# Sampled and end key blocks in one score product, weight tiles moved ahead in the queue, and an order planned by forward and backward passes

## The chip, the cores and the metric

The kernel runs on one core of one Trainium2 chip. The metric is the device time of one execution in microseconds. Before the change the median of three runs is 842.47 us (842.19 to 844.38).

## The reference

Block-sparse attention feeds a two-layer expert with a piecewise activation. There are 4 batches, 8 heads, 768 positions and a head size of 64. Positions form 24 blocks of 32. A query of block i attends to blocks i-1, i and i+1, to blocks 0 and 23, and to three blocks drawn for i. Queries of blocks 0 and 23 attend to everything.

```
scores = where(mask, q @ k.T / 8, -1e9)
attn   = softmax(scores);  x = attn @ v            # 3072 tokens x 512
h      = x @ w_in                                  # 512 -> 2048
g      = where(h >= 1, h, where(h <= -1, 0, (h + 1)**2 / 4))
out    = g @ w_out                                 # 2048 -> 512
```

The weights arrive in float64 and q, k, v in float32.

## The kernel before

**Groups.** Each batch is cut into six groups of 128 query rows. Groups 0 to 4 of a batch hold four middle blocks each; the sixth, called mixed, holds blocks 21 and 22 and the two dense blocks 0 and 23. There are 24 groups, 4 of them mixed. Groups are gathered into nine chunks of (3, 2, 3, 3, 3, 3, 3, 2, 2) groups; the expert (the MoE steps) of a chunk runs over its rows while the attention of the next chunk is worked in between.

**Attention of a group.** A middle group has two score rounds, a mixed one has one. So there are 20 x 2 + 4 = 44 rounds, of which the first two chunks (five middle groups) hold 10 and the other chunks 34. `score_parts` issues a round: 16 products (4 query blocks, 2 head halves `e`, 2 head pairs), each product of 32 queries on a 64-row by 32-column part of TensorE, so that eight parts work side by side, into the two PSUM banks `sa` and `sb`. Each product is made three times over: with the three neighbour blocks out of `KN` (96 columns), with the three sampled blocks out of `KR` (96 columns), and with blocks 0 and 23 out of `KN` (64 columns). A float32 product is two instructions, so each of the three sections is 32 matmuls. A bf16 product with `mask` follows. All go through the helper `mm` (L193). Then VectorE takes minima (L378), ScalarE exponentials (L381), TensorE turns the probabilities (`turn`, L386), and `values` multiplies them with the value tiles `VA` and `VB`. The rows of the mixed group that attend to everything get `far_scores` over all 24 blocks and `far_values`.

**Sampled blocks.** GpSimd reads three block numbers per query block into registers and copies the blocks from `KN` to one of three buffers `KR` (six copies of 128 x 128 for two query blocks, L321). SyncE reads the same numbers and loads the value blocks into `VA` (six transfers, L328). `KN` holds all keys of one batch and has one buffer.

**Weights.** `convert` loads a tile of 128 x 512 float64 into one of four parts of `STG`, and makes of it two float32r tiles (high and low part): ScalarE (L249), four VectorE instructions (L250, L252, L254, L256), a ScalarE copy (L258), a GpSimd subtraction (L260). There are 16 tiles of `w_in`, which stay, and 16 of `w_out`, which also go out to DRAM and come back in every later chunk. All 32 conversions belong to the time up to the end of chunk 0's MoE steps. A MoE step is twelve matmuls into `h` (L591 to L593), the activation on ScalarE, GpSimd and VectorE (L596 to L604), and three matmuls per group into `oa` (L610 to L612).

**The order.** Nothing is issued as it is written down. `Plan.add` records each step with its engine, an estimated duration and a key (a due time made of hand-set constants such as `T0`, `P0`, `CONV0` and the `LEAD_` values). `Plan.order` plays the steps through once: whenever an engine is free it takes the ready step with the smallest key. The order in which steps were taken is the order in which instructions are issued, on each engine and on SyncE's one queue of transfers.

Of the kernel before, what the change touches and what calls it, by code (L numbers as in the profile page):

```python
# [9 lines left out]
F32 = mybir.dt.float32  # L10
# [10 lines left out]
NB, BLK, NR = 24, 32, 3  # L21
# [12 lines left out]
class Plan:  # L34
# [24 lines left out]

    def order(self):  # L60

        n = len(self.steps)
        left = [len(s[4]) for s in self.steps]
        users = [[] for _ in range(n)]
        for i, s in enumerate(self.steps):
            for d in s[4]:
                users[d].append(i)
# [7 lines left out]
        done, wire, out, begin, fin = [], 0.0, [], [0.0] * n, [0.0] * n  # L75
        busy = {e: 0.0 for e in free}
        while len(out) < n:
            best = None
            for e in free:
                t = free[e]  # L80
                if e == "SP" and len(done) >= LANES:
                    t = max(t, done[-LANES])
                while wait[e] and wait[e][0][0] <= t:
                    i = heapq.heappop(wait[e])[1]
                    heapq.heappush(avail[e], (self.steps[i][2], i))
                if not avail[e]:
                    if not wait[e]:
                        continue
                    t = wait[e][0][0]
                if best is None or t < best[0]:  # L90
                    best = (t, e)
            t, e = best
            while wait[e] and wait[e][0][0] <= t:
                i = heapq.heappop(wait[e])[1]
                heapq.heappush(avail[e], (self.steps[i][2], i))
            i = heapq.heappop(avail[e])[1]
            eng, dur, key, fn, deps, lat, size = self.steps[i]
            begin[i] = t
            free[e] = t + dur
            busy[e] += dur  # L100
            end = t + dur + lat
            if size:
                wire = max(wire, t + dur + 1.0) + size / 290e3
                end = wire + 0.8
                if e == "SP":
                    done.append(end)
            out.append(i)
            fin[i] = end
            for u in users[i]:
                left[u] -= 1  # L110
                ready[u] = max(ready[u], end)
                if not left[u]:
                    heapq.heappush(wait[self.steps[u][0]], (ready[u], u))
        self.begin, self.fin, self.busy, self.end = begin, fin, busy, max(free.values())
        return out


LANES = 8


@with_exitstack
def body(ctx, tc, q_t, k_t, v, samp, moe_w_in, moe_w_out, cst_in, out):
# [148 lines left out]
    def group(b, t, key, wide, lead):  # L271
# [20 lines left out]
        def at(x):  # L292
            return key + wide * x
# [9 lines left out]
        for hf in range(nh):  # L303
            n = half[0] % 3
            half[0] += 1
            slots.append(n)
            i0 = blocks[2 * hf]
            if fresh.get(n) != b:
                fresh[n] = b
                for name, tl, blk in (("va", VA[n], 0), ("vb", VB[n], NB - 1)):  # L310
                    src = v[b * S + blk * BLK:b * S + (blk + 1) * BLK].unsqueeze(1).to_broadcast([BLK, 2, DM])
                    load(at(0) - lead + 2.0 + hf, tl[96:128], src, (), [(name, n, "g")], size=131072)

# [4 lines left out]

            def keys(n=n, values_of=values_of):
                for m, val in enumerate(values_of(mybir.EngineType.Pool)):  # L320
                    POOL.tensor_copy(out=KR[n][:, m // NR, m % NR:m % NR + 1], in_=KN[:, bass.ds(val, 1)])  # L321

            pool(1.39 + 6 * 0.34, at(0) - 1.5 + hf, keys, ["sreg"] + [("kn", s) for s in range(6)], [("kr", n)])

# [4 lines left out]

            add("SP", 0.3 + 6 * 0.42, at(0) - lead + 3.5 + hf, gather, ["sreg"], [("va", n)], size=6 * 65536)  # L330
            src = bass.AP(v.tensor, (b * S + (i0 - 1) * BLK) * DM, [[DM, 96], [BLK * DM, 2], [1, DM]])
            load(at(0) - lead + 2.5 + hf, VB[n][0:96], src, (), [("vb", n)], size=393216)
        pool(0.75, at(0) - 0.5, lambda: POOL.tensor_scalar(out=q, in0=q, scalar1=-SCALE, scalar2=0.0, op0=ALU.mult, op1=ALU.add),
# [4 lines left out]

        kn_r = [("kn", s) for s in (range(6) if mixed else {0, 5, t, t + 1})]
        kr_r = [("kr", n) for n in slots]  # L340

        def score_parts(items):
# [11 lines left out]
            for e, p, col, quad, qs, i, c in items:  # L354
                go(e, quad, keys_at(col + 128, 3), q[64 * e:64 * e + 64, p, qs], KN[64 * e:64 * e + 64, i - 1:i + 2, p])
            for e, p, col, quad, qs, i, c in items:
                n, j = place(c)
                go(e, quad, keys_at(col, 3), q[64 * e:64 * e + 64, p, qs], KR[n][64 * e:64 * e + 64, j, :, p])
            for e, p, col, quad, qs, i, c in items:
                go(e, quad, lambda o: o[:, col:col + 256].rearrange("p (a s k) -> p a s k", a=2, k=BLK)[:, :, 3],  # L360
                   q[64 * e:64 * e + 64, p, qs], KN[64 * e:64 * e + 64, 0:NB:NB - 1, p])
            for e, quad, i in sorted({(x[0], x[3], x[5]) for x in items}, key=lambda x: (x[1], x[0])):
# [7 lines left out]
                if i in (1, NB - 2):  # L370
                    go(e, quad, both(4 if i == 1 else 6, 1), ones[es], never[es].unsqueeze(1).unsqueeze(2).to_broadcast([64, 2, 1, BLK]))

        score_reads = [qr, "mask", "ones"] + kn_r + kr_r
        va_r = [r for n in slots for r in (("va", n), ("va", n, "g"))]
        vb_r = [r for n in slots for r in (("vb", n), ("vb", n, "g"))]

# [20 lines left out]
        if not mixed:  # L397
            for rnd in range(2):
# [11 lines left out]
                for a in range(2):  # L410
                    p = 2 * rnd + a
                    bn, bk = ptbank()
                    pe(0.4, at(0.28 * rnd + 0.12 + 0.1 * a),
                       lambda a=a, bk=bk: turn(bk, [P[2 * a + e][:, h * 128:h * 128 + 128] for e in range(2) for h in range(2)]),
# [3 lines left out]
            def values():  # L418
                first = True
                for p in range(NP):  # L420
                    for e in range(2):
                        for hf in range(2):
                            for c in range(4):
                                n, j = place(c)
# [4 lines left out]
            pe(2.2, at(0.66), values, [("pt", p) for p in range(NP)] + va_r + vb_r, [on])  # L429

# [5 lines left out]
        else:  # L436
# [9 lines left out]
            for rho in range(2):  # L446
                pe(0.4, at(0.10 + 0.05 * rho),
                   lambda rho=rho: turn(ptb, [P[2 * rho + e][:, h * 128:h * 128 + 128] for e in range(2) for h in range(2)]),
# [3 lines left out]
            def near_values():  # L452
                first = True
                for rho in range(2):
                    for e in range(2):
                        for hf in range(2):
                            for u in range(2):
                                hd = 2 * (rho + 2 * u) + e
                                for c in range(2):
                                    n, j = place(c)  # L460
                                    quad = 2 * u + c
# [3 lines left out]

            pe(1.25, at(0.25), near_values, [("pt", 0), ("pt", 1)] + va_r + vb_r, [on])

# [81 lines left out]

        pe(0.4, k0 + 0.02 * wide, turn_back, ["xn", "cst"], [bn])  # L550
        pv = bk.rearrange("p (a c) -> p a c", a=NP)
# [12 lines left out]
    def moe(c, t0, p):  # L564
# [5 lines left out]
        for fi in range(NF):  # L570
# [23 lines left out]

            pe(0.7 * size[c], u, l1, x_r + [(("wi", fi // 4, k), w_) for k in range(4) for w_ in ("hi", "lo")], [hn])
            act(0.6, u, lambda r=r, h=h: ACT.activation(out=r, in_=h, func=AF.Relu, bias=half_c, scale=0.5),  # L596
# [16 lines left out]

            pe(0.7 * size[c], u + p * L2, l2, [("gh", n3), ("gl", ng)] + w_r, [("oa", t) for t in range(size[c])])
        for t in range(size[c]):
# [14 lines left out]

    fresh = {}
    constants()
# [9 lines left out]
    for c in range(NC):  # L642
# [93 lines left out]
```

## Time and profile before

| | |
|---|---|
| median of three runs | 842.47 us |
| the profiled execution's own time | 842.23 us |
| its span, first to last instruction | 840.4 us |
| TensorE matmul busy | 769.2 us, 92% |
| VectorE busy | 404.6 us, 48% |
| ScalarE busy | 387.5 us, 46% |
| GpSimd busy | 212.6 us, 25% |

The own time is 1.83 us above the span; the rest of the document counts in the span's microseconds from its start. Shares are means over stages with different limits, so the table says little on its own: the stages have to be read apart. PE stands for TensorE, DVE for VectorE, ACT for ScalarE, POOL for GpSimd, and SP (its queue: SPq) for SyncE.

### The profile page before, as it was taken

To read this page: it belongs to the slowest core of one execution; us is meant where nothing else is said; L and a number is where in the kernel's file an instruction comes from. 1 tells how busy PE (TensorE), PEld (TensorE's weight loads), DVE (VectorE), ACT (ScalarE), POOL (GpSimd) and SP (SyncE) were. 2 spreads that over 40 slices of the span, in tenths; PEclk is the share of its full clock that TensorE was granted. 3 is DMA by queue.
4 is the path that set the end of the run, shared out by engine and by line. 5 is a ranking of instruction groups with operands and counts; after the bars stand their busy time and mean duration, and the time that the engine had idled before them with its cause. 6 is when DMAs were issued, how large, how long until landed. Compare 5 with 4: busy or idle time off the path is not lost.

```text
span 840.4 us, 27419 instructions
## 1 busy us (share of the span) xinstructions
PE 769.2 (92%) x11376; PEld 665.4 (79%) x11376; DVE 404.6 (48%) x781; ACT 387.5 (46%) x959; POOL 212.6 (25%) x468
## 2 busy tenths in 40 slices
PE   4467669999989899999999999999999999999996
PEld 3356548788877788888888888888888798887995
DVE  2377989884454334434444344434433243444322
ACT  1365746555453334363435434364434343445542
POOL 2255464531422121014222111014223030110110
PEclk6598979999999999999999999999999999999999
DMA  6667779679656545666454745665454636353554
GB/s 189 214 179 224 236 221 330 232 250 298 218 182 168 176 143 170 194 217 195 122 161 150 223 137 165 200 216 195 134 175 159 187 111 195 125 166 121 160 196 151
DMA packets 63280, 157.24 MB, mean 187 GB/s; under 512 B 9652, under 2 KB 9908, under 8 KB 63156
## 3 DMA queue, kind: packets, MB, share of 16 engines
q1 hardware_dynamic: 63156, 155.49, 58.9%
q8 instruction: 89, 1.46, 0.7%
q14 instruction: 35, 0.29, 0.1%
HBM read 140.78 MB, written 14.68 MB: 185 GB/s over the span
## 4 chain that ended last, share of the span: by engine, by line
PE 78%; DVE 7%; DMA 4%; issue 4%; SPq 3%; ACT 2%; POOL 1%; ACTq 0%; POOLq 0%; DVEq 0%
PE h L591 10%; PE oa L610 10%; PE oa L611 10%; PE oa L612 9%; PE h L593 9%; PE h L592 9%; PE ob L193 6%; PE ptb L386 5%; PE sa L193 5%; PE sb L193 2%; SPq L328 2%; DVE stg L254 1%; DVE stg L256 1%; DMA va<-in_v_dram 1%; DMA stg<-in_moe_w_in_dram 1%
## 5 line engine op out<-in xcount | busy, mean ns | idle before, releaser
L598 POOL TENSOR_SCALAR gt<-r 128x384 f32<-128x384 f32 (+1 forms) x144 | 72.9, 506 | 480.6 <-ACT r L596 459.2
L591 PE MATMUL h<-x,wi 128*128 128x384 f32 (+1 forms) x536 | 182.3, 340 | 4.4 <-ACT r L596 2.9
L593 PE MATMUL h<-x,wi 128*128 128x384 f32 (+1 forms) x536 | 172.2, 321 | 0.0
L592 PE MATMUL h<-x,wi 128*128 128x384 f32 (+1 forms) x536 | 171.8, 321 | 0.0
L610 PE MATMUL oa<-w,gh 128*128 128x512 f32 x384 | 158.2, 412 | 10.0 <-ACT w L258 6.6
L611 PE MATMUL oa<-w,gh 128*128 128x512 f32 x384 | 153.6, 400 | 1.1 <-POOL w L260 1.1
L612 PE MATMUL oa<-w,gl 128*128 128x512 f32 x384 | 153.0, 399 | 0.0
L601 DVE SCALAR_TENSOR_TENSOR r<-r,gt 128x384 f32<-128x384 f32 (+1 forms) x144 | 77.3, 537 | 121.9 <-ACT r L600 121.4
L604 DVE TENSOR_TENSOR gl<-r,gh 128x384 fp32r<-128x384 f32 (+1 forms) x144 | 78.5, 545 | 119.2 <-PE oa L612 99.6
L603 ACT CAST gh<-r 128x384 fp32r<-128x384 f32 (+1 forms) x144 | 68.7, 477 | 118.1 <-DVE r L601 95.5
L591 PEld LDWEIGHTS h<-x,wi 128*128 128x128 f32 x536 | 101.0, 188 | 17.8 <-ACT r L596 5.9
L596 ACT ACTIVATE r<-h,half_c 128x384 f32<-128x384 f32 (+1 forms) x134 | 73.8, 551 | 88.9 <-PE h L593 84.1
L592 PEld LDWEIGHTS h<-x,wi 128*128 128x128 f32 x536 | 101.3, 189 | 2.0 <-issue 1.0
L593 PEld LDWEIGHTS h<-x,wi 128*128 128x128 f32 x536 | 101.0, 188 | 0.0
L600 ACT ACTIVATE r<-r 128x384 f32<-128x384 f32 (+1 forms) x144 | 70.4, 489 | 59.0 <-POOL gt L598 58.5
L610 PEld LDWEIGHTS oa<-w,gh 128*128 128x128 f32 x384 | 73.5, 191 | 25.1 <-ACT w L258 6.8
L321 POOL COPY kr<-kn 128x128 f32 x264 | 74.0, 329 | 60.7 <-PE sb L193 31.9
L612 PEld LDWEIGHTS oa<-w,gl 128*128 128x128 f32 x384 | 73.5, 191 | 16.5
L611 PEld LDWEIGHTS oa<-w,gh 128*128 128x128 f32 x384 | 73.7, 192 | 13.7 <-POOL w L260 2.0
L193 PE MATMUL sa<-kn,q 64*32 64x96 f32 (+2 forms) x1408 | 66.7, 259 | 5.9 <-issue 2.7
L381 ACT ACTIVATE p<-sa,nm 128x256 f32<-128x256 f32 x84 | 39.3, 471 | 68.6 <-DVE nm L378 66.0
L193 PE MATMUL sb<-kn,q 64*32 64x96 f32 (+2 forms) x1408 | 65.7, 259 | 0.0
(112 smaller groups left out, 1172.7 us busy)
## 6 DMA issues: line engine op xcount, KB each, us to landing
w<-wo_dram SPq DMA_DIRECT2D x128, 512.0 KB, 3.5
vb<-in_v_dram SPq DMA_DIRECT2D x44, 384.0 KB, 3.9
va<-in_v_dram SPq DMA_DIRECT2D x264, 64.0 KB, 2.8
stg<-in_moe_w_in_dram SPq DMA_DIRECT2D x16, 512.0 KB, 5.0
stg<-in_moe_w_out_dram SPq DMA_DIRECT2D x16, 512.0 KB, 4.2
wo_dram<-w SPq DMA_DIRECT2D x16, 512.0 KB, 4.6
q<-in_q_t_dram SPq DMA_DIRECT2D x24, 256.0 KB, 4.2
kn<-in_k_t_dram SPq DMA_DIRECT2D x24, 256.0 KB, 4.6
```

The costliest lines, as they stand in the source:

```text
L193: PE.matmul(out=o, lhsT=l, rhs=r, start=start, stop=True, skip_group_check=True)
L321: POOL.tensor_copy(out=KR[n][:, m // NR, m % NR:m % NR + 1], in_=KN[:, bass.ds(val, 1)])
L591: PE.matmul(out=h, lhsT=wi[:, j, 0, fs], rhs=x[:, j, 0, 0:nt], start=(j == 0), stop=False)
L592: PE.matmul(out=h, lhsT=wi[:, j, 0, fs], rhs=x[:, j, 1, 0:nt], start=False, stop=False)
L593: PE.matmul(out=h, lhsT=wi[:, j, 1, fs], rhs=x[:, j, 0, 0:nt], start=False, stop=(j == NP - 1))
L596: act(0.6, u, lambda r=r, h=h: ACT.activation(out=r, in_=h, func=AF.Relu, bias=half_c, scale=0.5), [hn, "half_c"], [("r", n2)])
L598: pool(0.55, u, lambda r=r, gt=gt: POOL.tensor_scalar(out=gt, in0=r, scalar1=2.0, scalar2=-1.0, op0=ALU.mult, op1=ALU.add), [("r", n2)], [ ...
L601: dve(0.56, u, lambda r=r, gt=gt: DVE.scalar_tensor_tensor(out=r, in0=r, scalar=1.0, in1=gt, op0=ALU.min, op1=ALU.max), [("gt", n2)], [("r ...
L604: dve(0.56, u, lambda r=r, gh=gh, gl=gl: DVE.tensor_tensor(out=gl, in0=r, in1=f(gh), op=ALU.subtract), [("r", n2), ("gh", n3)], [("gl", ng)])
L610: PE.matmul(out=oa[t], lhsT=gh[:, ts], rhs=w[:, 0], start=(fi == 0), stop=False)
L611: PE.matmul(out=oa[t], lhsT=gh[:, ts], rhs=w[:, 1], start=False, stop=False)
L612: PE.matmul(out=oa[t], lhsT=gl[:, ts], rhs=w[:, 0], start=False, stop=(fi == NF - 1))
```

## The change

It has three parts.

First, `KR` gets two more places: blocks 0 and 23 are copied beside the three sampled ones (`ends`, two copies of 128 x 256 whenever a buffer goes to another batch), and the sampled product and the product with blocks 0 and 23 become one of 160 columns. It is issued first, the neighbour product second. `KR` goes from three buffers to two. The value rows move to match: block 23 stands at the head of `VB` and the neighbours behind it. Numbers and sizes of transfers stay.

Second, the constants of the keys are set anew. `CONV0` goes from 7.6 to -20 and the lead of the first chunk's attention loads from 60 to 18.45, so that by the keys the first four `w_in` tiles come ahead of the first group's loads. Some estimated durations change too.

Third, `order` plays the steps through up to five times. After each forward pass a backward pass runs from the end to the start and gives every step a new key (how late it may begin); the forward pass with the earliest planned end is kept.

```diff
-    def order(self):
+    def run(self, key, deps, back):
...
+    def order(self):
+
+        deps = [s[4] for s in self.steps]
+        users = [set() for _ in deps]
+        for i, d in enumerate(deps):
+            for x in d:
+                users[x].add(i)
+        key, best = [s[2] for s in self.steps], None
+        for _ in range(PASSES):
+            got = self.run(key, deps, False)
+            if best is None or got[0] < best[0]:
+                best = got
+            ends = [-(got[2][i] + s[1]) for i, s in enumerate(self.steps)]
+            key = [-x for x in self.run(ends, users, True)[3]]
+        self.end, out, self.begin, self.fin = best
...
-    KR = ring(3, [128, 2, NR, NP, BLK], F32, "kr")
+    KR = ring(2, [128, 2, NR + 2, NP, BLK], F32, "kr")
...
-        add("SP", 0.35 * n, key, lambda: SP.dma_start(out=dst, in_=src), reads, writes, size=size)
+        add("SP", 0.47 * n, key, lambda: SP.dma_start(out=dst, in_=src), reads, writes, size=size)
...
+            if stale.get(kn) != b:
+                stale[kn] = b
+
+                def ends(kn=kn):
+                    for j in range(2):
+                        POOL.tensor_copy(out=KR[kn][:, j, NR:NR + 2], in_=KN[:, 0:NB:NB - 1])
+
+                pool(0.9, at(0) - 1.6 + hf, ends, [("kn", 0), ("kn", 5)], [("kr", kn, "g")])
...
             for e, p, col, quad, qs, i, c in items:
-                go(e, quad, keys_at(col + 128, 3), q[64 * e:64 * e + 64, p, qs], KN[64 * e:64 * e + 64, i - 1:i + 2, p])
+                (n, kn), j = place(c)
+                go(e, quad, keys_at(col, NR + 2), q[64 * e:64 * e + 64, p, qs], KR[kn][64 * e:64 * e + 64, j, :, p])
             for e, p, col, quad, qs, i, c in items:
-                n, j = place(c)
-                go(e, quad, keys_at(col, 3), q[64 * e:64 * e + 64, p, qs], KR[n][64 * e:64 * e + 64, j, :, p])
-            for e, p, col, quad, qs, i, c in items:
-                go(e, quad, lambda o: o[:, col:col + 256].rearrange("p (a s k) -> p a s k", a=2, k=BLK)[:, :, 3],
-                   q[64 * e:64 * e + 64, p, qs], KN[64 * e:64 * e + 64, 0:NB:NB - 1, p])
+                go(e, quad, keys_at(col + 160, 3), q[64 * e:64 * e + 64, p, qs], KN[64 * e:64 * e + 64, i - 1:i + 2, p])
...
-                group(b, t, A0 + k * A1, A2, 60)
+                group(b, t, A0 + k * A1, A2, LEAD_0)
...
-T0, P0, P1, P2, PM, PA = 38.0, 90.0, 67.0, 44.93, 13.0, 7.52
-A0, A1, A2 = -4.19, 9.4, 6.84
-CONV0 = 7.6
+T0, P0, P1, P2, PM, PA = 35.99, 96.44, 67.0, 40.35, 11.57, 3.32
+A0, A1, A2 = -4.19, 14.61, 6.84
+CONV0 = -20
...
-LEAD_C, LEAD_I, LEAD_O, LEAD_W, LEAD_A, AHEAD = 10.52, 19.03, 13.7, 9.0, 14.41, 7.63
-L2 = 3.07
+LEAD_0, LEAD_C, LEAD_I, LEAD_O, LEAD_W, LEAD_A, AHEAD = 18.45, 15.26, 17.12, -1.85, 6.51, 14.41, 7.63
+L2 = 2.54
```

## Rows read from the trace of the kernel before

**Rows 1.** The page: span, and busy tenths of PE in 40 slices.
```profile
span 840.4 us, 27419 instructions
...
PE   4467669999989899999999999999999999999996
```
**Rows 2.** Windows by stage: width, busy of PE, PEld, DVE, ACT, POOL, clock, DMA share, GB/s.
```profile
0.00:6.00 6.00, 4.58 (x16) 4.25 (x16) 0.43 (x4) 1.28 (x1) 0.20 (x4) 1.00 0.27 77
6.00:33.60 27.60, 8.72 (x220) 5.78 (x220) 5.90 (x16) 2.52 (x9) 8.63 (x32) 0.54 0.79 220
33.60:76.30 42.70, 29.68 (x1068) 23.93 (x1068) 31.00 (x56) 26.57 (x76) 19.25 (x42) 0.82 0.67 209
76.30:118.56 42.26, 26.18 (x661) 22.06 (x662) 39.98 (x60) 26.40 (x63) 25.74 (x22) 0.90 0.76 227
118.56:174.50 55.94, 54.35 (x252) 46.83 (x253) 52.21 (x80) 34.07 (x70) 27.82 (x25) 0.95 0.78 259
174.50:205.00 30.50, 30.36 (x297) 24.18 (x296) 17.99 (x45) 16.02 (x35) 5.89 (x9) 1.00 0.90 275
205.00:833.80 628.80, 613.72 (x8859) 537.36 (x8858) 256.42 (x523) 280.03 (x706) 125.09 (x337) 0.99 0.55 173
```
**Rows 3.** Timelines of SP's queue and ACT, first 46 us: start, us, instruction.
```profile
2.24 0.43 SPq L190 DMA_DIRECT2D q<-in_q_t_dram  x1
...
29.25 1.88 SPq L190 DMA_DIRECT2D stg<-in_moe_w_in_dram  x4
...
33.63 0.66 ACT L249 ACTIVATE stg<-stg 128x512 f32<-128x512 f32 x1 [11.12 <-DMA stg<-in_moe_w_in_dram]
```
**Rows 4.** Groups by line and form: VectorE's part of a weight conversion.
```profile
L256 DVE SCALAR_TENSOR_TENSOR stg<-stg 128x512 int32<-128x512 int32 x32 | 27.3, 852 | 0.1
L254 DVE SCALAR_TENSOR_TENSOR stg<-stg 128x512 int32<-128x512 int32 x32 | 26.8, 837 | 0.3
...
L252 DVE TENSOR_SCALAR stg<-stg 128x512 int32<-128x512 int32 x32 | 21.0, 660 | 0.2
...
L250 DVE TENSOR_SCALAR stg<-stg 128x512 f32<-128x512 f32 x32 | 18.0, 569 | 13.1 <-ACT stg L249 13.1
```
**Rows 5.** PE timeline of one score round: first matmul of each section.
```profile
312.63 0.27 PE L193 MATMUL sa<-kn,q 64*32 64x96 f32 x1
...
312.99 0.24 PE L193 MATMUL sa<-kr,q 64*32 64x96 f32 x1
...
313.32 0.22 PE L193 MATMUL sa<-kn,q 64*32 64x64 f32 x1
...
313.67 0.25 PE L193 MATMUL sa<-mask,ones 64*32 64x192 bf16 x1
...
313.95 0.45 PE L591 MATMUL h<-x,wi 128*128 128x384 f32 x1
```
**Rows 6.** PE timeline of one far-score step: first two matmuls of one part.
```profile
352.75 0.53 PE L193 MATMUL sa<-kn,q 64*64 64x384 f32 x1
...
353.13 0.48 PE L193 MATMUL sa<-kn,q 64*64 64x384 f32 x1
```
**Rows 7.** Groups by line and form: the products with blocks 0 and 23.
```profile
L193 PE MATMUL sa<-kn,q 64*32 64x64 f32 x672 | 27.7, 235 | 2.7 <-issue 2.7
```
**Rows 8.** The chain from 205 to 833.8 us: start, us, what; its two longest stalls.
```profile
249.85 4.07 issue
...
273.08 2.80 issue
```
**Rows 9.** Groups by line and form: POOL's copies and its scaling of q.
```profile
L321 POOL COPY kr<-kn 128x128 f32 x264 | 74.0, 329 | 60.7 <-PE sb L193 31.9 <-issue 13.4 <-DMA vb<-in_v_dram 5.5
...
L333 POOL TENSOR_SCALAR q<-q 128x512 f32<-128x512 f32 x24 | 15.9, 661 | 26.1 <-DMA q<-in_q_t_dram 25.8
```
**Rows 10.** POOL timeline at a change of batch.
```profile
381.34 1.75 POOL L321 COPY kr<-kn 128x128 f32 x6 [1.27 <-issue]
383.54 1.49 POOL L321 COPY kr<-kn 128x128 f32 x6 [0.45 <-issue]
```

More of the change, by code (lines that the diff above doesn't have):

```diff
@@ L58, in add @@
         return n
-    def order(self):
+    def run(self, key, deps, back):
         n = len(self.steps)
-        left = [len(s[4]) for s in self.steps]
+        left = [len(d) for d in deps]
         users = [[] for _ in range(n)]
-        for i, s in enumerate(self.steps):
-            for d in s[4]:
-                users[d].append(i)
+        for i, d in enumerate(deps):
+            for x in d:
+                users[x].append(i)
         ready = [0.0] * n
@@ L74, in order @@
                 heapq.heappush(wait[self.steps[i][0]], (0.0, i))
-        done, wire, out, begin, fin = [], 0.0, [], [0.0] * n, [0.0] * n
-        busy = {e: 0.0 for e in free}
+        done, wire, issue, out, begin, fin = [], 0.0, 0.0, [], [0.0] * n, [0.0] * n
         while len(out) < n:
@@ L80, in order @@
                 t = free[e]
-                if e == "SP" and len(done) >= LANES:
+                if e == "SP" and not back and len(done) >= LANES:
                     t = max(t, done[-LANES])
@@ L84, in order @@
                     i = heapq.heappop(wait[e])[1]
-                    heapq.heappush(avail[e], (self.steps[i][2], i))
+                    heapq.heappush(avail[e], (key[i], i))
                 if not avail[e]:
@@ L94, in order @@
                 i = heapq.heappop(wait[e])[1]
-                heapq.heappush(avail[e], (self.steps[i][2], i))
+                heapq.heappush(avail[e], (key[i], i))
             i = heapq.heappop(avail[e])[1]
-            eng, dur, key, fn, deps, lat, size = self.steps[i]
+            dur, lat, size = self.steps[i][1], self.steps[i][5], self.steps[i][6]
             begin[i] = t
[L99 to L103, printed above, removed]
+            end = free[e] = t + dur
+            if size and back:
+                wire = max(wire, t + 0.8) + size / RATE
+                free[e] = wire - 0.8
+                end = issue = max(issue, wire + 1.0) + dur
+            elif size:
+                wire = max(wire, end + 1.0) + size / RATE
                 end = wire + 0.8
-                if e == "SP":
-                    done.append(end)
+                done.append(end)
+            elif not back:
+                end += lat
             out.append(i)
@@ L110, in order @@
                 left[u] -= 1
-                ready[u] = max(ready[u], end)
+                ready[u] = max(ready[u], end + (self.steps[u][5] if back and not self.steps[u][6] else 0.0))
                 if not left[u]:
                     heapq.heappush(wait[self.steps[u][0]], (ready[u], u))
-        self.begin, self.fin, self.busy, self.end = begin, fin, busy, max(free.values())
+        return max(free.values()), out, begin, fin
+    def order(self):
+        deps = [s[4] for s in self.steps]
+        users = [set() for _ in deps]
+        for i, d in enumerate(deps):
+            for x in d:
+                users[x].add(i)
[7 more added lines that the diff above has]
+        self.end, out, self.begin, self.fin = best
+        self.busy = {e: sum(s[1] for s in self.steps if s[0] == e) for e in ("PE", "ACT", "DVE", "POOL", "SP")}
         return out
-LANES = 8
+LANES, RATE, PASSES = 8, 310e3, 5
 @with_exitstack
@@ L303, in group @@
         for hf in range(nh):
-            n = half[0] % 3
+            n, kn = half[0] % 3, half[0] % 2
             half[0] += 1
-            slots.append(n)
+            slots.append((n, kn))
             i0 = blocks[2 * hf]
@@ L317, in values_of, with keys @@
                     skip_runtime_bounds_check_because="the sampled numbers are numbers of key blocks")[1]
-            def keys(n=n, values_of=values_of):
+            if stale.get(kn) != b:
[4 more added lines that the diff above has]
+                pool(0.9, at(0) - 1.6 + hf, ends, [("kn", 0), ("kn", 5)], [("kr", kn, "g")])
+            def keys(kn=kn, values_of=values_of):
                 for m, val in enumerate(values_of(mybir.EngineType.Pool)):
-                    POOL.tensor_copy(out=KR[n][:, m // NR, m % NR:m % NR + 1], in_=KN[:, bass.ds(val, 1)])
-            pool(1.39 + 6 * 0.34, at(0) - 1.5 + hf, keys, ["sreg"] + [("kn", s) for s in range(6)], [("kr", n)])
+                    POOL.tensor_copy(out=KR[kn][:, m // NR, m % NR:m % NR + 1], in_=KN[:, bass.ds(val, 1)])
+            pool(1.39 + 6 * 0.34, at(0) - 1.5 + hf, keys, ["sreg"] + [("kn", s) for s in range(6)], [("kr", kn)])
             def gather(n=n, values_of=values_of):
@@ L337, in place @@
             return slots[c // 2], c % 2
-        kn_r = [("kn", s) for s in (range(6) if mixed else {0, 5, t, t + 1})]
-        kr_r = [("kr", n) for n in slots]
+        kn_r = [("kn", s) for s in (range(6) if mixed else (t, t + 1))]
+        kr_r = [r for _, kn in slots for r in (("kr", kn), ("kr", kn, "g"))]
         def score_parts(items):
@@ L370, in score_parts @@
                 if i in (1, NB - 2):
-                    go(e, quad, both(4 if i == 1 else 6, 1), ones[es], never[es].unsqueeze(1).unsqueeze(2).to_broadcast([64, 2, 1, BLK]))
+                    go(e, quad, both(5 if i == 1 else 7, 1), ones[es], never[es].unsqueeze(1).unsqueeze(2).to_broadcast([64, 2, 1, BLK]))
         score_reads = [qr, "mask", "ones"] + kn_r + kr_r
-        va_r = [r for n in slots for r in (("va", n), ("va", n, "g"))]
-        vb_r = [r for n in slots for r in (("vb", n), ("vb", n, "g"))]
+        va_r = [r for n, _ in slots for r in (("va", n), ("va", n, "g"))]
+        vb_r = [r for n, _ in slots for r in (("vb", n), ("vb", n, "g"))]
         def reduce(e, col):
@@ L427, in values @@
                             first = False
-            pe(2.2, at(0.66), values, [("pt", p) for p in range(NP)] + va_r + vb_r, [on])
+            pe(2.4, at(0.66), values, [("pt", p) for p in range(NP)] + va_r + vb_r, [on])
             def recip():
@@ L593, in l1 @@
                     PE.matmul(out=h, lhsT=wi[:, j, 1, fs], rhs=x[:, j, 0, 0:nt], start=False, stop=(j == NP - 1))
[L595 removed]
+            pe(0.71 * size[c], u, l1, x_r + [(("wi", fi // 4, k), w_) for k in range(4) for w_ in ("hi", "lo")], [hn])
             act(0.6, u, lambda r=r, h=h: ACT.activation(out=r, in_=h, func=AF.Relu, bias=half_c, scale=0.5),
@@ L612, in l2 @@
                     PE.matmul(out=oa[t], lhsT=gl[:, ts], rhs=w[:, 0], start=False, stop=(fi == NF - 1))
-            pe(0.7 * size[c], u + p * L2, l2, [("gh", n3), ("gl", ng)] + w_r, [("oa", t) for t in range(size[c])])
+            pe(0.71 * size[c], u + p * L2, l2, [("gh", n3), ("gl", ng)] + w_r, [("oa", t) for t in range(size[c])])
         for t in range(size[c]):
```

22 lines of the change are left out of this document (11 added, 11 removed).

## The prediction, made before the result was known

> **What bounds the kernel now.** I read the page's slices first: TensorE is busy at 9 tenths nearly everywhere except in the first six of 40 slices, of 21 us each [rows 1]. So I cut the span into stages and read each engine's busy time in each [rows 2]. Three regimes come out.
>
> From 205 to 833.8 us TensorE is busy 613.72 of 628.8 us, so only 15.1 us are idle, and VectorE is at 41%. This stage is as long as TensorE's own work. Only less work there, or less of the 15.1 us, shortens it. Of the 15.1 us two waits that the chain calls "issue" take 4.07 and 2.80 us [rows 8]; no operand is late in them.
>
> From 118.56 to 174.5 us, chunk 0's MoE steps, TensorE is busy 54.35 of 55.94 us, but VectorE also 52.21, or 93% [rows 2]. Both are full. VectorE does the activation and what is left of the weight conversions.
>
> Before 118.56 us neither is full. TensorE is busy 4.58 + 8.72 + 29.68 + 26.18 = 69.2 us, much of it at the lower clock (granted 0.54 of full from 6 to 33.6 us). VectorE is busy 0.43 + 5.90 + 31.00 + 39.98 = 77.3 us, so it is idle for 41.2, of which 5.6 before 6 us, 21.7 from 6 to 33.6, 11.7 up to 76.3 and 2.3 after [rows 2]. The reason for the 21.7 is in the queue: SP issues the first four weight tiles at 29.25 us, behind the loads of two groups, and ScalarE starts on the first at 33.63, after 11.12 us of waiting for that transfer [rows 3]. A conversion costs VectorE 0.569 + 0.660 + 0.837 + 0.852 = 2.92 us [rows 4], and 32 of them 93.4 us, the largest part of what VectorE does before 174.5 us. An early VectorE gap is therefore paid back at the end of chunk 0.
>
> **The order at the start.** The weight work stays as it is; it begins earlier. If the first tile is issued where SP now issues its first load of q, at 2.24 us, and takes the same 4.38 us from issue to ScalarE's start (29.25 to 33.63) [rows 3], conversions begin at 6.6 us and not at 33.6. VectorE then has up to 21.7 us of idle time to fill in that stretch. I do not take all of it. There are four staging parts; one comes free only after the whole chain of a conversion, and the same SP queue must get the first group's keys and values out. I take five conversions, 5 x 2.92 = 14.6 us, and 2.4 us of the 11.7 idle up to 76.3 us, since a tile that is done early cannot be waited for later: 17 us. What is late next is the attention of the first groups, whose loads now queue behind four tiles. That is hidden as long as VectorE has conversions to do, as it is the fuller engine; without that cover the attention is late by the four tiles' issue, 1.88 us [rows 3], and by their 2 MB on the wire, 9.5 us at 220 GB/s [rows 2].
>
> The bounds are these. Below, 0: the loads of tiles and of groups only change places, and chunk 0's steps still start when the later of both is there. Above, the transfers: up to 174.5 us they move 77 x 6 + 220 x 27.6 + 209 x 42.7 + 227 x 42.26 + 259 x 55.94 = 39.5 MB (GB/s times us, over 1000) [rows 2]. At the highest rate of any stage, 275 GB/s at a share of 0.90, that is 144 us, so no more than 30 us can be gained. At 259 GB/s it is 153 us, or 22 us gained. So 17 stands a little under what the transfers allow.
>
> **The score product.** In the round shown the sections begin at 312.63 (neighbours), 312.99 (sampled), 313.32 (blocks 0 and 23) and 313.67 us (mask) [rows 5]. The two that become one take 0.33 + 0.35 = 0.68 us. The section of 64 columns takes as long as one of 96, so at 64 columns something other than columns sets the pace, while at 96 columns may do. For 32 matmuls of 160 columns I have three prices: 0.35 us if columns never count; 0.345 x 160/96 = 0.575 if they count from 96 up (0.345 is the mean of 0.36 and 0.33); and by the far scores, where the second matmul of a part starts 0.38 us after the first for 384 columns [rows 6], four turns of 160/384 x 0.38, or 0.63 us. I take 0.575, since it comes from the same tiling: 0.68 - 0.575 = 0.105 us saved a round. The form has 672 matmuls into `sa` and as many into `sb`, 16 of each a round, so 42 rounds, and two rounds of the first chunk go to other banks [rows 7]: 44. Only those in the TensorE-bound stage count, 34 rounds of chunks 2 to 8: 34 x 0.105 = 3.6 us, with bounds 34 x 0.05 = 1.6 and 34 x 0.33 = 11.2. The other ten fall where TensorE waits anyway.
>
> One rule speaks against this part. The row shows 0.33 and 0.36 us for 32 matmuls of 96 columns, each with its own weight load in the same part, so the load seems hidden [rows 5]. The Trainium skill ("TensorE: Matmul & The Clock Gate", Part 3: Packing small matmuls — row/col tiling) says that a weight load overlaps a running matmul only when it goes to another row group; here successive loads of a part share its rows. By that page's 32/1.2 = 27 ns a load, four turns would add an estimated 0.11 us to the streaming and leave hardly 0.05 us of saving a round, 1.6 us in all, and the forecast would be 2 us higher. By that rule, the trace does not agree at 96 columns: a turn takes 0.345/4 = 0.086 us, less than the 0.095 us that the far scores' 0.38 us for 384 columns would give it, load included [rows 5, 6].
>
> **Copies, buffers, queue.** `ends` adds 2 copies x 2 buffers x 4 batches = 16 copies on GpSimd, each between 0.329 us (128 columns) and 0.661 us (512 columns) [rows 9], so some 0.45 us for 256 and 7.2 us in all. I cost them at nothing: GpSimd is idle for 80% of the long stage [rows 2], and its sampled copies wait 31.9 us for TensorE's score rounds as it is [rows 9]. At a change of batch they stand in a chain (keys, copies, scores) that the MoE steps cover; without the cover it would be three times 1.8 us, 5.4 us. With two `KR` buffers both halves of a group's copies wait for the last score round of the group before, and now the first product of a round needs them. At 381.34 us the two halves take until 385.03, 3.7 us [rows 10]. Groups follow each other by some 629/19 = 33 us in the long stage, so this is hidden too; see the second rival. SP issues as many transfers as before, of the same sizes.
>
> **The new order later on.** Two plans of the same work differ in the waits that they leave. 15.1 us of idle time is all that a better order can take there; a worse one can add, and the nearest row is the longest stall of 4.07 us [rows 8], of which two or three more would be 10. I take no change, and keep -15 to +10.
>
> **The sum.** 840.4 - 17 - 3.6 = 819.8 us of span, 821.6 us with the 1.83 us around it. The profiled execution is 0.24 us under the median of the runs shown, so 822 us.
>
> **The rivals.** (a) The start gains nothing much: tiles and groups trade places, or the pass that is kept has lost the early tiles again, and 0 to 5 us come of it. The first stage then is bound by both inputs, and GpSimd's and ScalarE's parts wait as before. The time is 842.5 - 3.6 - (0 to 5), 834 to 839; say 836. For it: up to 33.6 us transfers already have a share of 0.79 at 220 GB/s [rows 2]. Against it: that share falls to 0.67 right after, while VectorE still has 11.7 us idle.
>
> (b) Slower: with two `KR` buffers, and keys that say how late a step may begin, the sampled copies of a group come just before its first round, and TensorE waits for them at the first product. The price is up to 3.7 us a group [rows 10]. Half of that for the 19 groups of the long stage is 35 us, and the time 822 + 35 = 857. It decides from (17 + 3.6)/19 = 1.1 us a group on. For it: the sampled product used to come second, behind 0.36 us of other work. Against it: 33 us between groups.
>
> (c) The order also removes most of the 15 us of idle time late, say 11, or the transfers carry a start gain near 30: 793 to 808, say 805. For it: nothing in rows 8 is a late operand that an order must leave. Against it: nothing in the plan knows of such waits.
>
> **Chances.** The forecast 0.58 (its own range 808 to 834), (a) 0.22, (b) 0.10, (c) 0.10. About 0.3%, 2.5 us, is what a measurement of this kernel can tell from no change, so faster means under 840. The forecast, (c) and three quarters of (a) are faster: 0.58 + 0.10 + 0.16 = 0.84. The rest of (a) is the same: 0.06. (b) is slower: 0.10. The range 801 to 839 leaves out (b), a fifth of (a) and half of (c): some 0.19.
>
> **What would show it.** The start is right if the first `stg` transfer is issued before 4 us, ScalarE's L249 begins near 7, and VectorE's idle time before the first L610 falls from 41 to about 24 us, with chunk 0 ending some 17 us earlier. The product is right if a round's 160-column section lasts 0.55 to 0.63 us and the whole round about 1.2 in place of 1.32. (b) shows as TensorE waiting for POOL at L193, and (a) as VectorE idle near 40 us before chunk 0 with the wait moved to attention's loads. The prediction is wrong if the stage after chunk 0 changes by more than 10 us in either direction, since I take its order's worth as nothing.

## The result and the profile after

The changed kernel takes 812.01 us in the median of four runs (809.75 to 816.68), the kernel before 842.49 us beside it: a ratio of 0.9641, with a 95% interval of 0.9593 to 0.9688. The forecast was 822 us, 10 us too long, within its own range of 808 to 834. The span of the profiled execution fell from 840.4 to 811.6 us, by 28.8. Three readings say where.

**The start.** Page of the kernel after, span and busy tenths of PE (compare [rows 1]), and then its windows by stage, with the columns of [rows 2]; here the first step into `oa` comes at 93.60 us:

```profile
span 811.6 us, 24505 instructions
...
PE   4666999999989999999999999999999999999997
```

```profile
6.00:33.60 27.60, 13.45 (x274) 9.03 (x278) 17.31 (x38) 10.84 (x28) 16.15 (x33) 0.59 0.86 253
33.60:76.77 43.17, 26.58 (x691) 20.41 (x682) 34.48 (x56) 24.30 (x64) 24.24 (x36) 0.70 0.84 243
76.77:93.60 16.83, 16.36 (x209) 14.65 (x209) 13.19 (x23) 10.85 (x29) 9.58 (x17) 0.82 0.75 218
93.60:118.56 24.96, 23.74 (x303) 20.16 (x301) 24.96 (x37) 15.64 (x35) 15.58 (x18) 1.00 0.60 186
118.56:165.95 47.39, 45.02 (x423) 37.33 (x423) 46.34 (x75) 31.04 (x70) 23.61 (x21) 1.00 0.86 292
...
205.00:805.40 600.40, 592.85 (x7545) 519.80 (x7544) 249.61 (x510) 273.74 (x688) 120.69 (x322) 1.00 0.56 175
```

VectorE works 17.31 us from 6 to 33.6 us, where it worked 5.90 [rows 2], and the transfers' share there rises from 0.79 to 0.86. VectorE is full (24.96 of 24.96 us) from 93.60 us on. The first MoE step into `oa` starts 23.2 us earlier, at 93.59 us instead of 116.82, although the first into `h` starts no earlier (76.77 against 76.33). The chain of waits over the first 100 us of the kernel after names what limits it there:

```profile
6.50 7.88 DMA stg<-in_moe_w_in_dram
14.40 9.04 DMA vb<-in_v_dram
...
47.49 6.93 DMA vb<-in_v_dram
54.50 6.93 DMA stg<-in_moe_w_in_dram
61.50 4.38 DMA stg<-in_moe_w_in_dram
```

Transfers of weights and of values alternate in it, at a share of 0.84 to 0.86.

Chunk 1's first product into `h` starts at 165.95 us instead of 174.92, only 9 us earlier, and chunk 0's last product into `oa` at 176.50 instead of 189.09, 12.6 us earlier: steps of both chunks and of attention run among each other there. So I take a mark that means the same amount of MoE work in both kernels: the point where TensorE has done 288 matmuls into `h` and 174 into `oa`, at 209.7 us before and 197.6 after. That is 12.1 us earlier, and the kernel after has one more score round, 1.22 us, behind it by then. The start gave 13.3 us.

**The score round.** TensorE's timeline of one round after (compare [rows 5]): the new section of 160 columns, the neighbours, the mask, the next step.

```profile
293.11 0.32 PE L212 MATMUL sa<-kr,q 64*32 64x160 f32 x1
...
293.67 0.24 PE L212 MATMUL sa<-kn,q 64*32 64x96 f32 x1
...
294.00 0.24 PE L212 MATMUL sa<-mask,ones 64*32 64x192 bf16 x1
...
294.33 0.50 PE L635 MATMUL oa<-w,gh 128*128 128x512 f32 x1
```

The section lasts 293.67 - 293.11 = 0.56 us, the round 1.22 us instead of 1.32: 0.10 us saved.

**The long stage.** From 205 us on TensorE is idle for 600.40 - 592.85 = 7.55 us, where it was idle for 15.1 [rows 2]. Of the chain from 205 to 805.4 us after, these are the stalls, each with the piece ahead of it where that is among the longest (before 389.03 a score round of short pieces stands between; compare [rows 8]):

```profile
212.79 1.57 PE ob L212 x101
214.37 1.40 issue
...
232.75 1.80 PE ob L212 x118
234.55 2.08 issue
...
385.95 1.92 PE ob L212 x128
389.03 1.24 issue
...
442.80 0.94 issue
...
574.71 0.94 issue
```

The longest stall is 2.08 us, where there were 4.07 and 2.80. By the waits of the two traces, the stalls shrank from 11.7 to 7.0 us in all (with one of 0.38 us that is not shown), and the waits for a `w` tile from 2.5 to 0.6. No long wait for a `w` tile is left before 802 us. Before, such waits also cost clock. Two windows of the kernel before, right behind its stall at 249.85 us and its wait for `w` from 664.8 to 666.6 us:

```profile
253.90:257.90 4.00, 3.98 (x38) 3.24 (x39) 0.86 (x2) 0.00 (x0) 0.00 (x0) 0.58 0.41 115
666.60:670.60 4.00, 3.99 (x24) 2.79 (x32) 0.58 (x2) 0.34 (x1) 0.00 (x0) 0.57 0.47 187
```

The granted clock there is 0.58 and 0.57, with TensorE busy throughout: most of each window at 1.2 GHz instead of 2.4. That is 4 x 0.42 + 4 x 0.43 = 3.4 us lost. After, the granted clock is 1.00 over the whole long stage.

The account: start 13.3, columns of 33 rounds after the mark 3.3, idle time 7.5, clock 3.4; together 27.5 of 28.8 us. The end behind the last matmul gives 0.4, and 0.9 is not assigned.

### The profile page after: what moved, and what is told of

Its sections match the earlier page's. It is cut to its first block, busy times and chain, and to the rows that moved or that the text cites. A ratio compares the mean times of both kernels' runs of the same rounds, so it can differ in the third digit from the quotient of the medians.

```text
span 811.6 us, 24505 instructions
## 1 busy us (share of the span) xinstructions
PE 763.1 (94%) x9968; PEld 659.8 (81%) x9968; DVE 402.9 (50%) x781; ACT 387.5 (48%) x959; POOL 221.5 (27%) x484
## 4 chain that ended last, share of the span: by engine, by line
PE 81%; DMA 7%; DVE 7%; issue 3%; SPq 1%; ACT 1%; POOL 0%; POOLq 0%; ACTq 0%; DVEq 0%
PE oa L635 10%; PE h L616 10%; PE oa L637 10%; PE oa L636 10%; PE h L618 9%; PE h L617 9%; PE ob L212 6%; PE ptb L411 5%; PE sa L212 5%; DMA vb<-in_v_dram 3%; DMA stg<-in_moe_w_in_dram 3%; PE sb L212 2%; DVE stg L273 1%; DVE stg L275 1%; PE ptb L572 1%
## 5 line engine op out<-in xcount | busy, mean ns | idle before, releaser
L637 PE MATMUL oa<-w,gl 128*128 128x512 f32 x384 | 151.1, 393 | 0.0
L349 POOL COPY kr<-kn 128x128 f32 x264 | 79.7, 347 | 48.4 <-PE sb L212 30.0
L635 PEld LDWEIGHTS oa<-w,gh 128*128 128x128 f32 x384 | 72.3, 188 | 15.7 <-issue 3.0
L417 DVE COPY pt<-ptb 128x512 f32<-128x512 f32 x70 | 48.3, 690 | 70.8 <-PE ptb L411 70.7
L636 PEld LDWEIGHTS oa<-w,gh 128*128 128x128 f32 x384 | 72.5, 189 | 12.4 <-POOL w L279 1.5
L411 PE MATMUL ptb<-cst,p 128*128 128x128 f32 x328 | 51.7, 282 | 1.4 <-DVE x L578 1.0
```

The lines of the kernel that those rows point to most:

```text
L349: POOL.tensor_copy(out=KR[kn][:, m // NR, m % NR:m % NR + 1], in_=KN[:, bass.ds(val, 1)])
L411: PE.transpose(out=bank[:, k * 128:k * 128 + 128], in_=s, identity=ident)
L635: PE.matmul(out=oa[t], lhsT=gh[:, ts], rhs=w[:, 0], start=(fi == 0), stop=False)
L636: PE.matmul(out=oa[t], lhsT=gh[:, ts], rhs=w[:, 1], start=False, stop=False)
L637: PE.matmul(out=oa[t], lhsT=gl[:, ts], rhs=w[:, 0], start=False, stop=(fi == NF - 1))
```

## The experiments

Ratios are to the kernel before, run on the same chip. "Start" is the time of the mark above, read from one profiled execution of each kernel; "stalls" are the chain's issue waits after 205 us. In three runs the order has done other attention steps by the mark than the kernel that the run is compared with; there the start is also given on equal work, with a score round counted at 1.22 us, the `far_values` of a mixed group at 1.55 and four transposes at 0.36.

**The product alone taken back**, in the order of the kernel after. In `score_parts`:

```diff
-  go(e, quad, keys_at(col, NR + 2), q[...], KR[kn][..., j, :, p])
+  go(e, quad, keys_at(col, NR), q[...], KR[kn][..., j, 0:NR, p])
+for e, p, col, quad, qs, i, c in items:
+  (n, kn), j = place(c)
+  go(e, quad, keys_at(col + 96, 2), q[...], KR[kn][..., j, NR:NR + 2, p])
```

> The order of the changed kernel is kept step for step; only the 160-column product is issued as two again, 96 sampled columns and 64 end columns, both out of the copies. If the product is worth its columns alone, 34 rounds of 0.10 us come back and the time is 812 + 3.4 = 815 to 816, with the waits that the chain calls issue unchanged. Rival: the later waits went away because a round has 64 instructions fewer (104 to 72 matmuls, each with its weight load); then the waits called issue come back too, some 8 us more, and the time is 822 to 826.

Measured: 822.18 us, ratio 0.9716 (0.9674 to 0.9758), in the rival's range; the interval just touches the changed kernel's. In the traces the last matmul comes 8.2 us later (814.90 against 806.66): 1.2 at the start, 7.0 after, of which columns are about 3.3. The rest is stalls, seven of over 0.4 us instead of five, and clock. Two neighbouring windows of this run, the columns as before:

```profile
376.50:380.50 4.00, 1.86 (x111) 1.78 (x111) 1.25 (x2) 0.29 (x1) 2.34 (x10) 1.00 0.65 197
380.50:384.00 3.50, 3.50 (x13) 2.67 (x12) 1.75 (x3) 1.13 (x4) 0.62 (x3) 0.60 0.11 42
```

A gap of 2.1 us, and the clock falls to 0.60 right behind it. So in this order the product is worth more than its columns, by way of the stalls.

**One pass instead of five** (`PASSES` 5 to 1), with the new keys and product.

> The changed kernel with the first forward pass alone, so the order of the new keys without the backward passes. If the new keys brought the earlier start and the passes only reorder later work, the time stays within 5 us of 812 and the first step into oa begins near 94 us. Rival: the passes bring the start; then that step begins at 110 us or later and the time is 825 to 838, no better than the product and some waits make it.

Measured: 821.87 us, ratio 0.9705 (0.9665 to 0.9745); first `stg` transfer at 2.70 us, first step into `oa` at 98.62, start 207.6, or 207.3 on equal work. With one pass the keys do put weights first, and in the traces that order is slower at the start by 9.7 us than the one kept after the passes. (This profiled execution took 826.21 us, 4.3 more than the median of its four, so the usual difference may be smaller.)

**The old key constants**, with five passes and the new product (`LEAD_0 = 60`, `CONV0 = 7.6` and the others of before).

> The changed kernel with all key constants of before and the five passes. If the passes forget the keys that they start from, the time is 812 to 818 and the first weight tile is issued before 10 us as in the changed kernel. Rival: the keys decide, the first tile is issued near 29 us again, and the time is 825 to 838.

Measured: 816.76 us, ratio 0.9657 (0.9618 to 0.9697); first `stg` at 11.22 us, start 201.0, or 200.3 on equal work, 2.7 later than in the changed kernel; part of that is made up behind it. The interval overlaps the changed kernel's: once passes run, the new constants make no difference in the whole time that these runs can tell.

**Passes alone**, in the kernel before (its durations, keys and product; the new `run` and `order`).

> The kernel before with the forward and backward passes alone: its product in three parts, three copy buffers, its keys and its estimated durations and rate. If the order is worth what the profile after shows (13.5 us at the start, 11 later) and the passes need no new durations, 816 to 820. Rival: the passes need the corrected durations of SP's issues (0.47 for 0.35 us a transfer, 4.5 for 2.8 us a gather), since they squeeze the start around them; then 828 to 840.

Measured: 830.02 us, in the rival's range, ratio 0.9809 (0.9768 to 0.9849); first `stg` at 9.96 us, start 203.6 instead of 209.7. A wait for `w` of 4.18 us stays in the chain at 651.73.

**The product alone**, with planner, durations and keys of before.

> The kernel before with the product part alone (160 columns, copies of blocks 0 and 23, two buffers), its keys, durations and single forward pass. If the product is worth its columns, 34 rounds of 0.10 us plus a few us of waits called issue: 3 to 7 us less than before, a ratio of 0.992 to 0.996. Rival: with two buffers and the copies needed first, TensorE waits for POOL at the first product; then no gain or a loss, a ratio of 0.998 to 1.01.

Measured: 836.96 us, ratio 0.9905 (0.9871 to 0.9938), a little under the first expectation, with the start at 217.8, or 215.9 on equal work, 6.2 us later than before. TensorE's waits for the first 130 us show the two buffers' price, once, at the start:

```profile
PE sa L193 <- POOL kr L330: 8.0, 2, 7.3
```

Yet the last matmul is 7.1 us earlier (827.96 against 835.05): no stall is longer than 1.53 us, where there were 4.07 and 2.80, without any change of the planner. So the product alone made the work from the mark on 13.3 us shorter: 5.9 of idle time, 3.4 of clock, and columns for most of the rest.

**Passes and corrected durations**, product and keys of before (`0.47 * n` a load, `1.4 + 6 * 0.51` a gather, `RATE` 310e3 and the TensorE durations).

> The kernel before with the passes and the corrected durations and rate (a transfer's issue 0.47, a gather 4.5, 310 GB/s), without the product and with the old keys. If the corrected durations are what the passes alone lacked, the start is as in the changed kernel (first step into oa near 95 to 99 us, not 110) and the ratio is 0.970 to 0.975. Rival: the durations do nothing, and the passes alone stay at 0.981.

Measured: 824.49 us, ratio 0.9754 (0.9707 to 0.9801); first step into `oa` at 103.99 us, between the two expectations, and start 200.1. By the medians the durations add 0.55% to passes alone, though the intervals overlap; 3.5 us of it are at the start.

**Hardly any reload.** What are the stalls? One candidate is the data's transfers, which would hold up TensorE's instructions. This run reloads only 8 of the 1024 values of each row of `w_out` tiles after chunk 0, and leaves the rest of the tile as it was.

```diff
-  load(..., f(W[s].rearrange("p a d -> p (a d)")), f(wo_dram[fi]), ...)
+  load(..., f(W[s][:, 0, 0:8]), f(wo_dram[fi][:, 0:8]), ...)
```

> The changed kernel, step for step in the same order, but the reloads of w_out tiles from DRAM in chunks 1 to 8 bring 8 of 1024 values a row and leave the rest as it was; 128 transfers of 512 KB shrink to 4 KB. If the waits called issue are instructions that arrive late because the data transfers are in their way, the waits after 205 us fall from 7.0 us to under 2, and the time by 4 to 8 us, with the last wait for a tile. Rival: the instructions come too slowly by themselves where small matmuls stand close together; then the waits stay at 5 to 8 us and the time falls by 3 us at most.

Measured: 811.34 us, ratio 0.9607 (0.9563 to 0.9652). Its long stage, and its stalls in the chain:

```profile
205.00:798.00 593.00, 588.31 (x7527) 516.41 (x7526) 250.03 (x507) 272.55 (x685) 121.05 (x322) 1.00 0.26 72
```

```profile
214.90 1.40 issue
...
235.09 0.98 issue
...
388.08 0.80 issue
...
572.00 1.51 issue
```

The share of the transfers fell from 0.56 to 0.26. Four of the five stalls stand at the same places, 4.7 us in all instead of 7, and the time is 2.1 us below that of the changed kernel in the next run, which the intervals do not tell apart. So busy transfer engines may account for a third of the stalls, but the rest is there without them.

**The changed kernel once more**, on the same chip as the three runs ahead of it.

> The changed kernel once more, beside the others on the same chip: a ratio of 0.962 to 0.967 as before, as the mark for the other three.

Measured: 813.43 us, ratio 0.9636 (0.9592 to 0.9681), stalls of 1.12, 1.81, 0.97, 1.67 and 1.07 us at the same places as in the kernel after. They belong to the place in the instruction stream; their lengths vary.

**Score and values steps kept apart.** In the kernel after, four of the five stalls stand where a score round and a values step, both of small matmuls, follow each other on TensorE. Here the finished order is edited: wherever the two are neighbours and a MoE step comes next, the MoE step goes between them, if nothing that it needs comes later.

```diff
-    seq = plan.order()
+    seq = plan.apart(plan.order())
...
+  if {kind(a), kind(b)} == {"score", "value"} and kind(c) == "moe":
+      out.remove(c); out.insert(at[b], c)
```

> The changed kernel, but wherever TensorE's order has a score round and a values step of the attention back to back, the next MoE step is put between them (four places, all of them where the traces after show a wait called issue of 1 to 2 us). If such waits are instructions that come too slowly for small matmuls close together, these four waits go, one near 442 us stays, and the time falls by 4 to 6 us: a ratio of 0.957 to 0.960. Rival: the waits are tied to something else, such as the block of instructions that is due; then they appear at other places, 5 to 7 us in all, and the ratio stays at 0.962 to 0.966.

Measured: 807.73 us (806.65 to 809.27), ratio 0.957 (0.9547 to 0.9594), the best version of the study. The long stage and the stalls that are left:

```profile
205.00:800.00 595.00, 592.91 (x7546) 519.25 (x7545) 249.46 (x509) 272.92 (x686) 120.25 (x320) 1.00 0.57 176
```

```profile
234.12 0.66 issue
...
437.86 0.75 issue
```

TensorE is idle for 2.1 us there; the kernel after, over the same window, for 7.0. Moving steps at four places took 5 us of stalls away, with all instructions and transfers the same.

**The same order with the product taken back**, the first experiment's edit upon the last one's.

> The same order, with the 160-column product as two again (96 and 64 columns out of the copies). If the product's worth beyond its 3.4 us of columns lay in waits called issue, the two kernels with steps apart differ by 3 to 5 us, less than the 8.2 us of TensorE's time by which the split kernel stood behind the changed one. Rival: the product is worth 6 us or more whatever the order.

Measured: 817.06 us, ratio 0.9683 (0.9657 to 0.9709), 9.3 us above the same order with the product. The last matmul comes 7.85 us later (808.42 against 800.57): 2.7 at the start (199.9 against 197.2) and 5.1 after, of which 3.3 columns and most of the rest stalls, one of 1.41 us at 370.91. So the product's worth beyond its columns stays in an order with few stalls.

**More traffic at the start.** Is the start bound by transfers? Each `w_in` tile brings another 256 KB, which nothing uses: 4.2 MB in all.

```diff
+  SP.dma_start(out=EX[n % 4], in_=src.bitcast(I32)[:, 0:512])   # beside each w_in tile's load
```

> The changed kernel in the same order, with a second transfer of 256 KB into an unused buffer behind each of the 16 w_in tiles: 4.2 MB more before about 100 us, 17 us at the 245 GB/s of that stage, and 16 more issues of some 0.4 us. If the start is now bound by the transfers, the first step into oa comes 10 to 17 us later and the time grows by as much, a ratio of 0.975 to 0.985. Rival: VectorE's conversions still bound it, and the extra bytes fit in between: under 4 us, a ratio under 0.969.

Measured: 824.35 us, ratio 0.9768 (0.9738 to 0.9798). In the traces the mark comes at 205.4 us, 7.7 later than in the changed kernel on this chip, and from there on both take the same time (609.0 and 608.8 us). The profiled execution is the fastest of its four, 821.16 us; by the medians the run is 10.9 us slower. The windows of this run and then of the kernel after, over the same stretch:

```profile
33.60:77.00 43.40, 29.86 (x748) 22.60 (x740) 29.94 (x51) 21.92 (x58) 20.95 (x34) 0.64 0.90 264
```

```profile
33.60:77.00 43.40, 26.81 (x691) 20.64 (x683) 34.71 (x57) 24.53 (x65) 24.24 (x36) 0.70 0.84 243
```

At 264 GB/s, 4.2 MB are 16 us on the wire; about half of it is seen at the mark and two thirds in the medians. The share went from 0.84 to only 0.90 and VectorE lost 4.8 us in this stretch: some room was left, and not enough. The ratio is in the range of the first expectation, the mark 2 us short of it: most of such an amount is not hidden. The 16 added issues also hold SP's queue for 6.2 us, so the run does not tell the wire from the queue.

## Why the prediction was right, and where it was off

**The start, 17 us forecast: 13.3.** The mechanism was right, VectorE's gap filled early and paid back in chunk 0, and it was the largest term. Before the first step into `oa` VectorE works 0.4 us up to 6 us and 17.3 + 34.5 + 13.2 in the stages shown, 65.4 of 93.6 us, and is idle for 28.2; the forecast was about 24, instead of 41. How it came about was not as I said. I took weights to go first; the first four `stg` transfers left at 6.03 us, not before 4, behind the loads of keys, and ScalarE began at 13.12, not near 7. Timelines of SP's queue and of ScalarE after (compare [rows 3]):

```profile
2.23 2.80 SPq L209 DMA_DIRECT2D kn<-in_k_t_dram  x6
6.03 3.43 SPq L209 DMA_DIRECT2D stg<-in_moe_w_in_dram  x4
```

```profile
13.12 0.67 ACT L268 ACTIVATE stg<-stg 128x512 f32<-128x512 f32 x1 [11.10 <-DMA stg<-in_moe_w_in_dram]
```

The runs also show that "weights first" is not enough, nor needed for most of it: on equal work the start came 3.6 us earlier than before with one pass, where the weights left at 2.70 us, and 10.6 us earlier with old keys and five passes, where they left at 11.22. Passes alone gave 6.1 us, and 9.6 with the corrected durations. I also expected the end of chunk 0 17 us earlier; its last products came 10 us (into `h`) and 12.6 us (into `oa`) earlier, as steps of the next chunk moved in there, so that was the wrong place to look.

**The product, 3.6 us forecast: 0.10 us a round, as forecast (0.105).** The section took 0.56 us, forecast 0.575. The Trainium skill ("TensorE: Matmul & The Clock Gate", Part 3: Packing small matmuls — row/col tiling) says that a weight load overlaps running matmuls only in another row group; by that rule the section would have lasted an estimated 0.63 us or more, and the trace does not agree. But the columns were not all of its worth. Taking it back cost 6.3 us by the ratios in the one order, where the intervals just touch, and 9.3 us in the other, where they stand apart. A round also has 32 matmuls fewer, 44 x 32 = 1408 in all, and with the product back there were more stalls.

**The late order, forecast "no change": the step that failed.** Beyond the columns the long stage gained 10.9 us (7.5 idle, 3.4 clock), inside the stated bound of -15 and not in the sum. The working had two flaws. It looked at the 15.1 us of idle time as something only an order could take, where the product took more of it: alone, with fewer small instructions, it left no stall above 1.53 us and made the stage 13.3 us shorter, where passes alone made it 6.4 shorter. And it priced a stall at its own length, while two gaps of before, of 4.07 and 1.83 us, cost another 1.7 us each at the lower clock behind them. Rival (c), given 0.10, named the idle time but put it down to the order ("most of the 15 us", "say 11"); 7.5 us of it went, half. The span came out 8.2 us under the forecast's 819.8: 10.9 more here, 3.7 less at the start, and 1 from the rest. That the two errors partly cancel is luck. The prediction's own sign, a stage after chunk 0 that changes by more than 10 us, was met: it changed by 15, of which 3.3 are columns. And in the chances, (a)'s 834 to 839 us lie all under the 840 that counts as faster, so its whole 0.22 belonged there, not three quarters.

**Copies and buffers, forecast at nothing: right.** The row of the copies of `ends` in the page's groups of the kernel after:

```profile
L343 POOL COPY kr<-kn 128x256 f32<-128x256 f32 x16 | 6.3, 432 | 11.9 <-DMA kn<-in_k_t_dram 11.9
```

432 ns each, forecast 450. TensorE waits for `kr` 5.6 us in two waits before 100 us, and never after 205 us: rival (b) did not occur. Rival (a), a start that trades places, did not occur either, though more traffic shows that transfers are near.

**What stays open.** The stalls are tied to neighbouring steps of small matmuls, shown by keeping the steps apart, and only in part to the load on the transfers, shown by the small reload. That TensorE waits there for its own instructions is shown by the places of the stalls in the traces (last section); what sets when a packet of instructions is asked for is not. Why one pass leaves a late start although its weights go first, and whether the wire or SP's queue limits the start, is open too.

## What to carry to other kernels

Where one engine is the bound, list its idle time by what comes before each gap: if no operand is late, count the engine's instructions from gap to gap (a fixed spacing points to the instruction stream), look which kinds of steps are neighbours, and put a step of few, long instructions between two of many short ones. A merged product is worth its columns and the instructions that it no longer issues; measure it in the whole kernel, and in two orders. Judge a change of order by a mark of equal work on the bounding engine, not by the end of a stage whose contents the order may change, and even out what else has been done by the mark.

## What the hardware showed that I had not expected

TensorE stalled for up to 4.07 us with no operand late, most often where a score round and a values step (128 matmuls in 1.92 us) follow each other. In the window from 249.9 to 253.9 us of the kernel before, which is one such stall, the queue of instructions moved one packet:

```profile
q8 instruction: 1, 0.02, 1.5%
```

Over the kernel the change cut these packets from 89 to 78 (queue, packets, MB, share of the engines' span; before, then after):

```profile
q8 instruction: 89, 1.46, 0.7%
q8 instruction: 78, 1.28, 0.7%
```

That is 16 KB a packet. TensorE's records (matmuls, weight loads and its sequencer's own) are 22872 before and 20061 after, 257 to a packet. Counted in order of start, the stalls of the kernel after stand at instructions 5314, 6082, 9665, 10177, 11714 and 15041, each 193 or 194 past a multiple of 256. So do all 66 stalls over 0.3 us after 205 us in the thirteen traces, whatever the order, and in each TensorE goes on 1.2 to 1.7 us after a packet of this queue has landed; it passes none of these places sooner. So it waits there for the next packet of its own instructions, and a values step with its loads, 256 instructions, uses one up in 1.92 us.

The Trainium skill ("Runtime: NRT & Kernel Launch", Instruction fetch mechanics) says that the boundary of a block of instructions is mostly hidden, because dispatch is slower than the refill. The trace agrees at 53 of the 59 places that the kernel after passes from 205 us on and not at the other six: 7 us were not hidden, and 5 of them went when long matmuls came between.

The stall of 2.08 us in the kernel after, in a window from 1 us ahead of it, and the window behind it:

```profile
233.60:237.60 4.00, 1.92 (x82) 1.58 (x71) 1.35 (x3) 2.12 (x9) 1.09 (x2) 1.00 0.07 29
236.60:240.60 4.00, 3.97 (x34) 3.58 (x35) 1.45 (x3) 0.90 (x3) 0.00 (x0) 1.00 0.41 121
```

The transfers' share around it is 0.07, so little else was moving. And the clock stays at 1.00 behind this gap, while it fell to 0.60 and 0.58 behind those of 2.1 us (the product taken back) and 4.07 us (the kernel before), and to 0.57 behind one of 1.83 us, the wait for `w`; behind the stall of 2.80 us in the kernel before it stayed at 1.00 as well. The length of one gap does not decide whether the clock falls; what does is not told by these runs.
